# Moving the copy of one bank of finished accumulators from VectorE to ScalarE

## The chip, the cores and the metric

The kernel runs on one core of one Trainium2 chip. The metric is the device time of one execution in microseconds, shown as the median of several runs. Engines are named as in the profile: PE is TensorE's matmul stream and PEld its weight loads, DVE is VectorE, ACT is ScalarE, POOL is GpSimd, and SP issues DMAs.

## What is computed

The reference is a chunked linear recurrence (4 sequences, 8 heads, 768 positions, head width 32, state width 16), followed by a feed-forward block with the gate h * cos(h):

```python
# per chunk of positions, for each sequence and head
L = exp(cum[i] - cum[j]) * causal          # decays, cum = cumsum(log a)
y = ((C @ B.T) * L) @ x  +  (C @ state) * exp(cum)
state = exp(sum(la)) * state + sum_j B[j] x[j] * exp(cum[-1] - cum[j])

X = y.transpose(0, 2, 1, 3).reshape(3072, 256)
h = X @ w_in                                # 256 x 2048
out = (h * cos(h)) @ w_out                  # 2048 x 256
```

All inputs and outputs are float32.

## The kernel before

The 768 positions are cut into 6 chunks of 128. A chunk holds 4 x 128 = 512 tokens. The feed-forward block of a chunk takes 16 steps, numbered n = 16c + f through the whole kernel. A written-out loop over n sets the order of the instructions on every engine; there is no scheduler that would move them. From the second chunk on, the tokens of a chunk are handled in two turns of 8 steps, u = 0 and u = 1, each with half of the tokens and all of the 2048 inner columns.

Step n runs these parts, in this order:

- `first(n)`: 8 matmuls on TensorE form hp (L519), 128 x 512 in one PSUM bank; two banks are used in turn, so hp of step n+2 reuses the bank of step n. ScalarE computes k, the rounded number of turns (L523), and VectorE w = hp/(2 pi) - k (L525).
- `gate(n)`: ScalarE's sine (L530).
- `gated(n)`: VectorE's product gT = hp * cos (L535), which frees hp's bank. GpSimd then forms differences gd of it (`differ`, L560 to L563). Between gate and gated, and behind gated, VectorE has work for the scan of the next chunk: decays (L345) and masks (L436).
- the sums of a finished turn, if the step before ended one (`unsummed`, L633).
- `second(n - 2)`: from chunk 1 on this is `seven`: the product with w_out by seven half-size products in place of eight (L616). It is queued on TensorE behind hp of step n.

The seven products of a turn accumulate over 8 steps in two PSUM banks named o, called lo and hi. Products 1, 2 and 6 go to lo, products 7, 5, 4 and 3 to hi; a step issues them in the order 1, 2, 6, 7, 5, 4, 3. There are two buffers under the name o in all, so the next turn writes the same two banks, and its first step may write each only when it has been copied out. After the last step of a turn, lo is copied to the SBUF tile ps by ScalarE (L625) and hi by VectorE (L626). On ScalarE the next instruction is k of the next step; on VectorE it is w of the next step. The sums over ps (L633) and two output DMAs (L636) follow one step later, behind gated of that step.

There are 9 such ends of a turn: at steps 25, 33, 41 and so on up to 89 of the loop. The first chunk and the last turn of the last chunk finish in another way (L584; L648 and L661) and copy nothing with L625 or L626.

Of the kernel before, what the change touches and what calls it, by code (L numbers as in the profile page):

```python
# [25 lines left out]
def kernel(  # L26
# [30 lines left out]
    V, ACT, G, PE = nc.vector, nc.scalar, nc.gpsimd, nc.tensor  # L57
# [28 lines left out]
    def bank(shape, name, tag):  # L86
        return psum.tile(shape, FP32, tag=tag, bufs=2, name=name)

    def pair(name):

        return psum.tile([P, 2, 4 * P], FP32, tag="scan", bufs=2, name=name)
# [127 lines left out]
    for b in range(NB):  # L219
# [4 lines left out]
        out=a_in, in_=a.rearrange("(u b) h (c p) -> (b h c) u p", u=NU, p=P))  # L224
# [276 lines left out]
    hp, turns, gT, o = {}, {}, {}, {}  # L501
    NJ = NF // 2

    def turn_of(n):

        c, f = divmod(n, NF)
        return (f % 2, f // 2) if c == 0 else divmod(f, NJ)
# [59 lines left out]
    def second(n):  # L567
        c, f = divmod(n, NF)
        if c > 0:
            seven(n)  # L570
            return
        u, j = turn_of(n)
        if j == 0:
            o[c, u] = bank([P, 2, DM], "o", "o")
        g = gT.pop(n)
        for e in range(2):
            for t in range(2):
                PE.matmul(o[c, u][:, t], lhsT=g[:, 2 * e + t], rhs=w_out[:, 2 * j + e],  # L578
                          start=(j == e == t == 0), stop=(j == NJ - 1 and e == 1),
                          skip_group_check=True)  # L580
        if j < NJ - 1:
            return
        ob = conv.tile([P, 2, DM], FP32, tag="last", bufs=3, name="ob")
        (ACT.copy if u else V.tensor_copy)(out=ob, in_=o[c, u])  # L584
        for s in range(2):
            nc.sync.dma_start(out=to_rows[2 * u + s, c], in_=ob[s * W:(s + 1) * W])

    def seven(n):

        c = n // NF  # L590
        u, j = turn_of(n)
        final = n >= NC * NF - NJ
        if j == 0:


            if final:
                lo, hi = (pair("o")[:, 0].rearrange("p (q m) -> p q m", m=P) for _ in range(2))
                mid = bank([P, 4, P], "o", "o")
                o[c, u] = (mid, lo, hi, {1: mid[:, 0], 6: mid[:, 1], 7: mid[:, 2], 5: mid[:, 3],
                                         2: lo[:, 0], 3: lo[:, 1], 4: hi[:, 0]})  # L600
            else:
                lo, hi = (bank([P, 4, P], "o", "o") for _ in range(2))
                o[c, u] = (lo, hi, {1: lo[:, 0], 6: lo[:, 1], 2: lo[:, 2], 7: hi[:, 0],
                                    5: hi[:, 1], 4: hi[:, 2], 3: hi[:, 3]})
        at = o[c, u][-1]
        g = gT.pop(n)
        if n == NC * NF - 1:
            last_step(g, *o[c, u][1:3])
            return
        d = gd.pop(n)  # L610
        w = {1: w4[:, j, 0, 0], 2: w4[:, j, 1, 0], 3: w4[:, j, 1, 1], 4: wd[3][:, j],
             5: wd[0][:, j], 6: wd[2][:, j], 7: wd[1][:, j]}
        a_ = {1: g[:, 0], 2: g[:, 2], 3: d[:, 3], 4: g[:, 3], 5: d[:, 0], 6: d[:, 2], 7: d[:, 1]}
        starts = (1, 2, 4) if final else (1, 7)
        for q in (1, 2, 6, 7, 5, 4, 3):
            PE.matmul(at[q], lhsT=a_[q], rhs=w[q], start=(j == 0 and q in starts),  # L616
                      stop=(j == NJ - 1), skip_group_check=True)
        if final and j == NJ - 2:
            shared(o[c, u][0])
        if j < NJ - 1:  # L620
            return

        sum_ = two.tile([P, 7, P], FP32, tag="sum", bufs=1, name="sum")
        ps = two.tile([P, 7, P], FP32, tag="ps", bufs=1, name="ps")
        ACT.copy(out=ps[:, 0:3], in_=o[c, u][0][:, 0:3])  # L625
        V.tensor_copy(out=ps[:, 3:7], in_=o[c, u][1])  # L626

        def rest():
            for dst, a_, b_ in ((sum_[:, 0:2], ps[:, 1:3], ps[:, 0:1]),
                                (sum_[:, 5:7], ps[:, 3:5], sum_[:, 0:1]),  # L630
                                (sum_[:, 3:5], ps[:, 5:3:-1], sum_[:, 5:6]),
                                (sum_[:, 2:3], ps[:, 6:7], sum_[:, 6:7])):
                V.tensor_tensor(out=dst, in0=a_, in1=b_.to_broadcast([P, dst.shape[1], P]),  # L633
                                op=ALU.add)
            for s in range(2):
                nc.sync.dma_start(out=to_rows[2 * u + s, c],  # L636
                                  in_=sum_[s * W:(s + 1) * W, 1:5].rearrange(
                                      "p (t h) m -> p t (h m)", t=2))

        unsummed.append(rest)  # L640
# [4 lines left out]
    def shared(mid):  # L645

        ps = two.tile([P, 7, P], FP32, tag="ps", bufs=1, name="ps")
        ACT.copy(out=ps[:, 0:4], in_=mid)  # L648
        add = dict(op=ALU.add)
        V.tensor_tensor(out=ps[:, 1], in0=ps[:, 1], in1=ps[:, 0], **add)  # L650
        V.tensor_tensor(out=ps[:, 4:6], in0=ps[:, 2:4],
                        in1=ps[:, 1:2].to_broadcast([P, 2, P]), **add)
        V.tensor_tensor(out=ps[:, 6], in0=ps[:, 4], in1=ps[:, 3], **add)

        shares_.update({0: ps[:, 0:6:5], 1: ps[:, 4:7:2]})

    def last_step(g, lo, hi):

        for t, acc in enumerate((lo, hi)):
            for e in range(2):  # L660
                PE.matmul(acc[:, 0:2], lhsT=g[:, 2 * e + t], rhs=w_out[:, NF - 2 + e],  # L661
                          start=False, stop=(e == 1), skip_group_check=True)
            ob = conv.tile([P, 2, P], FP32, tag="last", bufs=3, name="ob")
            V.tensor_tensor(out=ob, in0=acc[:, 0:2], in1=shares_[t], op=ALU.add)
            for s, eng in enumerate((nc.sync, nc.scalar)):
                eng.dma_start(out=to_rows[NB - 2 + s, NC - 1, :, t],
                              in_=ob[s * W:(s + 1) * W].rearrange("p h m -> p (h m)"))
# [28 lines left out]
    for dst, src in ((a_cut, cut), (a_all, la)):  # L696
        nc.sync.dma_start(
            out=dst.rearrange("(u b) h (c p) -> (b h c) u p", u=NU, p=P), in_=src)
# [63 lines left out]
    for n in range(NC * NF + LAG):  # L762
        c, f = divmod(n, NF)
# [75 lines left out]
```

## Time and profile before

| | |
|---|---|
| median of 4 runs | 380.81 us (380.80 to 381.57) |
| the profiled execution | 380.8 us, span 379.0 us, clock granted to TensorE 1.0 |
| TensorE busy | 373.1 us (98%) |
| VectorE busy | 279.9 us (74%) |
| ScalarE busy | 173.4 us (46%) |
| GpSimd busy | 213.4 us (56%) |
| copy of lo (L625, ACT, 128x384) | 9 x 0.458 us |
| copy of hi (L626, DVE, 128x512) | 9 x 0.679 us |
| a step of L519 on TensorE | 1.73 us for 8 matmuls |
| a step of L616 on TensorE | 1.56 us for 7 products (14 records), in most steps |

The span is the time from the first to the last instruction that the profile shows; the execution's own time has 1.8 us around it. A busy share is an average over the whole span. Matmuls overlap, so that the sum of their single durations is more than the time that a step takes. Times in the timeline count from the start of the span.

### The profile page before, as it was taken

The numbers are of one execution on the slowest core, as the hardware profiler recorded it, in microseconds if no ns is written. First come the engines' busy times: TensorE is split into PE (matmuls) and PEld (weight loads), VectorE is DVE, ScalarE is ACT, GpSimd is POOL, SyncE is SP. The second block draws the span as 40 slices with busy tenths as digits, with TensorE's granted clock in tenths as the row PEclk, the third lists the DMA queues.
The fourth block names the chain that finished last, engine by engine and source line by source line (L and its number), as shares of the span: only waits on it lengthen the run. The fifth ranks groups of instructions, "written<-read, shape, count | busy, mean of one in ns | idle before, by whom it ended". The sixth has DMA issues, their size and how long they took to land.

```text
span 379.0 us, 7680 instructions
## 1 busy us (share of the span) xinstructions
PE 373.1 (98%) x2980; PEld 330.2 (87%) x2980; DVE 279.9 (74%) x431; ACT 173.4 (46%) x303; POOL 213.4 (56%) x330
## 2 busy tenths in 40 slices
PE   8999999999999999999999999999999999999996
PEld 2578888889989999998999998899998999999995
DVE  8879999899689748967748986756986862554643
ACT  4877756444344434443434453424444433433442
POOL 6767565579864437673444683443675343454551
PEclk9999999999999999999999999999999999999999
DMA  7999889979230961420781340100010000010011
GB/s 82 264 257 272 244 215 134 166 99 170 82 108 19 150 59 58 136 74 2 85 71 55 83 122 6 42 2 2 1 30 3 9 20 2 0 29 0 2 28 29
DMA packets 106371, 30.42 MB, mean 80 GB/s; under 512 B 75520, under 2 KB 102240, under 8 KB 106336
## 3 DMA queue, kind: packets, MB, share of 16 engines
q1 hardware_dynamic: 106176, 29.81, 39.8%
q8 instruction: 23, 0.38, 0.5%
q10 hardware_dynamic: 160, 0.13, 0.1%
q14 instruction: 12, 0.10, 0.1%
HBM read 26.59 MB, written 3.34 MB: 79 GB/s over the span
## 4 chain that ended last, share of the span: by engine, by line
PE 96%; DVE 2%; POOL 1%; issue 0%; POOLq 0%
PE hp L519 43%; PE o L616 33%; PE o L578 7%; PE g L423 3%; PE y L457 3%; PE y L450 1%; PE tp L406 1%; PE a_ps L299 1%; PE warm L101 1%; PE g L374 1%; DVE mag L209 1%; POOL w_in L217 1%; PE o L661 1%; DVE mag L207 0%; PE s_ps L478 0%; PE l_ps L318 0%
## 5 line engine op out<-in xcount | busy, mean ns | idle before, releaser
L519 PE MATMUL hp<-yT,w_in 128*128 128x256 f32 x768 | 183.8, 382 | 0.6 <-POOL w_in L217 0.3
L519 PEld LDWEIGHTS hp<-yT,w_in 128*128 128x128 f32 x768 | 139.5, 190 | 21.5 <-issue 3.2
L560 POOL TENSOR_TENSOR gd<-gT 128x256 f32<-128x256 f32 x79 | 59.9, 758 | 104.9 <-DVE gT L535 79.5
L530 ACT ACTIVATE w<-w,quarter 128x512 f32<-128x512 f32 x96 | 69.3, 722 | 77.7 <-DVE w L525 77.5
L523 ACT ACTIVATE k<-hp 128x512 int32<-128x512 f32 x96 | 57.2, 596 | 103.7 <-PE hp L519 103.1
L525 DVE SCALAR_TENSOR_TENSOR w<-hp,k 128x512 f32<-128x512 f32 x96 | 65.7, 684 | 50.3 <-ACT k L523 50.1
L535 DVE TENSOR_TENSOR gT<-hp,w 128x512 f32<-128x512 f32 x96 | 65.2, 679 | 32.4 <-ACT w L530 27.2
L616 PE MATMUL o<-words,gd 128*128 128x128 f32 x474 | 66.9, 277 | 0.0
L616 PEld LDWEIGHTS o<-words,gd 128*128 128x128 f32 x474 | 59.8, 192 | 0.5
L345 DVE TENSOR_TENSOR_SCAN lam<-arow,unit 128x512 f32<-128x512 f32 x40 | 55.7, 1393 | 0.0
L563 POOL TENSOR_TENSOR gd<-gT,gd 128x128 f32<-128x128 f32 x79 | 48.1, 608 | 6.2
L616 PEld LDWEIGHTS o<-w_out,gT 128*128 128x128 f32 x316 | 46.9, 191 | 3.5
L616 PE MATMUL o<-w_out,gT 128*128 128x128 f32 x316 | 48.0, 274 | 0.0
L562 POOL TENSOR_TENSOR gd<-gT,gd 128x128 f32<-128x128 f32 x79 | 41.4, 524 | 6.2
L578 PE MATMUL o<-w_out,gT 128*128 128x256 f32 x128 | 30.3, 380 | 0.4 <-POOL w_out L217 0.4
L616 PE MATMUL o<-w_out,gd 128*128 128x128 f32 x158 | 30.6, 275 | 0.0
L616 PE MATMUL o<-words,gT 128*128 128x128 f32 x158 | 30.5, 275 | 0.0
L578 PEld LDWEIGHTS o<-w_out,gT 128*128 128x128 f32 x128 | 24.2, 190 | 4.0 <-POOL w_out L217 0.8
L436 DVE TENSOR_TENSOR m<-g,lam 128x512 f32<-128x512 f32 x40 | 25.6, 680 | 0.0
L616 PEld LDWEIGHTS o<-w_out,gd 128*128 128x128 f32 x158 | 24.0, 192 | 0.0
L616 PEld LDWEIGHTS o<-words,gT 128*128 128x128 f32 x158 | 24.0, 192 | 0.0
L633 DVE TENSOR_TENSOR sum<-ps,sum 128x256 f32<-128x256 f32 (+1 forms) x27 | 16.7, 645 | 0.6
(91 smaller groups left out, 281.3 us busy)
## 6 DMA issues: line engine op xcount, KB each, us to landing
arow<-a_cut SPq DMA_DIRECT2D x20, 512.0 KB, 4.0
words<-in_moe_w_in_dram SPq DMA_DIRECT2D x8, 512.0 KB, 5.6
words<-in_moe_w_out_dram SPq DMA_DIRECT2D x8, 512.0 KB, 8.8
out_dram<-sum SPq DMA_DIRECT2D x18, 128.0 KB, 2.5
xr<-in_x_dram SPq DMA_DIRECT2D x4, 512.0 KB
along<-a_all SPq DMA_DIRECT2D x20, 64.0 KB
xr<-in_x_dram SPq DMA_DIRECT2D x8, 128.0 KB
bc<-in_B_dram SPq DMA_DIRECT2D x4, 256.0 KB, 5.1
```

Of the source, the lines that this page charges most:

```text
L345: V.tensor_tensor_scan(out=lam[c, b][:, hs].rearrange("p h i -> p (h i)"), data0=rows_.rearrange("p h i -> p (h i)"), data1=unit.rearrange ...
L436: V.tensor_tensor(out=of[0], in0=g[q][:, :, s * 2 * P:(s + 1) * 2 * P], in1=of[1], op=ALU.mult)
L519: PE.matmul(to_[:, e], lhsT=w_in[:, k, fs], rhs=y[:, k, u], start=(k == 0), stop=(k == KT - 1), skip_group_check=True)
L523: ACT.activation(k, hp[n], AF.Copy, bias=0.25, scale=INV_2PI)
L525: V.scalar_tensor_tensor(out=w, in0=hp[n], scalar=INV_2PI, in1=k, op0=ALU.mult, op1=ALU.subtract)
L530: ACT.activation(cos, cos, AF.Sin, bias=quarter, scale=TWO_PI)
L535: V.tensor_tensor(out=gT[n], in0=hp.pop(n), in1=cos, op=ALU.mult)
L560: G.tensor_tensor(out=d[:, 0:2], in0=g[:, 1:2].to_broadcast([P, 2, P]), in1=g[:, 3::-3], op=ALU.subtract)
L562: G.tensor_tensor(out=d[:, 2], in0=g[:, 0], in1=d[:, 0], op=ALU.subtract)
L563: G.tensor_tensor(out=d[:, 3], in0=g[:, 2], in1=d[:, 2], op=ALU.subtract)
L578: PE.matmul(o[c, u][:, t], lhsT=g[:, 2 * e + t], rhs=w_out[:, 2 * j + e], start=(j == e == t == 0), stop=(j == NJ - 1 and e == 1), skip_gr ...
L616: PE.matmul(at[q], lhsT=a_[q], rhs=w[q], start=(j == 0 and q in starts), stop=(j == NJ - 1), skip_group_check=True)
```

## The change

The copy of hi is issued on ScalarE's queue right behind the copy of lo, and no longer on VectorE's queue. Shapes, tiles and the order of everything else stay. On TensorE, the product that first writes hi in the next turn (product 7) waits for ScalarE where it waited for VectorE; the order of instructions on TensorE, GpSimd and the DMA queue is unchanged. ScalarE has 9 instructions more, VectorE 9 fewer.

```diff
         sum_ = two.tile([P, 7, P], FP32, tag="sum", bufs=1, name="sum")
         ps = two.tile([P, 7, P], FP32, tag="ps", bufs=1, name="ps")
         ACT.copy(out=ps[:, 0:3], in_=o[c, u][0][:, 0:3])
-        V.tensor_copy(out=ps[:, 3:7], in_=o[c, u][1])
+        ACT.copy(out=ps[:, 3:7], in_=o[c, u][1])
 
         def rest():
```

## The prediction

> **What bounds the kernel now.** I read the page's busy shares and its chain by engine first, then the chain in order of time, then the timelines of single engines at the turn boundaries. The page says:
>
> ```profile
> PE 373.1 (98%) x2980; PEld 330.2 (87%) x2980; DVE 279.9 (74%) x431; ACT 173.4 (46%) x303; POOL 213.4 (56%) x330
> PE 96%; DVE 2%; POOL 1%; issue 0%; POOLq 0%
> ```
>
> TensorE is busy for 98% of the span and carries 96% of the chain, so the other engines matter only where they make TensorE wait. The nine copies that the change moves take 6.1 us of VectorE; taking them away is worth nothing by itself. The question is what TensorE loses to them. The chain in order of time (start, length, what) shows it:
>
> ```profile
> 113.23 1.56 PE o L616 x14
> 114.79 1.73 PE hp L519 x8
> 116.52 1.73 PE o L616 x14
> ...
> 148.28 1.71 PE o L616 x14
> ...
> 208.22 1.67 PE o L616 x14
> ...
> 327.57 1.56 PE o L616 x14
> ```
>
> One step of the second product (L616, 7 products recorded as 14 matmuls) takes 1.56 us. The first step after a finished turn takes more: 1.73 at 116.52, 176.46, 236.35 and 296.25, 1.71 at 148.28, 1.67 at 208.22 and 268.12. At 327.57 and 353.89, the last two of the nine boundaries, it takes 1.56. Where inside the step the time goes, TensorE's weight loads show, an ordinary step first and the step after the first boundary second:
>
> ```profile
> 113.40 0.75 PEld L616 LDWEIGHTS o<-words,gd 128*128 128x128 f32 x6
> ...
> 116.69 0.92 PEld L616 LDWEIGHTS o<-words,gd 128*128 128x128 f32 x6
> ```
>
> The six loads are two each for products 6, 7 and 5. Product 7 is the first to write the second bank, which the copy of L626 must have emptied. VectorE and ScalarE at that boundary:
>
> ```profile
> 115.76 0.68 DVE L535 TENSOR_TENSOR gT<-hp,w 128x512 f32<-128x512 f32 x1
> 116.36 0.68 DVE L626 COPY ps<-o 128x512 f32<-128x512 f32 x1
> 117.24 0.69 DVE L525 SCALAR_TENSOR_TENSOR w<-hp,k 128x512 f32<-128x512 f32 x1 [0.20 <-ACT k L523]
> ```
> ```profile
> 114.68 0.72 ACT L530 ACTIVATE w<-w,quarter 128x512 f32<-128x512 f32 x1 [0.76 <-DVE w L525]
> 115.31 0.46 ACT L625 COPY ps<-o 128x384 f32<-128x384 f32 x1
> 116.61 0.60 ACT L523 ACTIVATE k<-hp 128x512 int32<-128x512 f32 x1 [0.84 <-PE hp L519]
> ```
>
> The turn's last matmul ends at 114.79. ScalarE empties its bank by 115.77. VectorE is still busy with masks and the product gT, begins its copy only at 116.36 and ends at 117.04. The load of product 7 starts at 117.09, 0.05 later; by the spacing of the loads (0.11) it would have started at 116.91. At all seven long boundaries that load starts about 0.05 behind the end of L626. At 327.57 the copy ends at 327.84, 0.12 ahead of the load, and nothing is lost.
>
> **The change part by part.**
>
> *Removed from VectorE:* 9 copies of 0.68 us. VectorE's next instruction, w (L525), starts at 117.24, 0.03 after ScalarE's k ended (116.61 + 0.60), and so at each boundary: it waits for k, not for VectorE. Nothing on that chain comes earlier: 0. The sum below takes no gain from VectorE's free time.
>
> *Added to ScalarE:* 9 copies of 128x512 from a bank of accumulators. The nearest row is ScalarE's own copy of the same kind in the last turn (L648), 0.587 us; the other 128x512 ScalarE copies are 0.565 (L584) and 0.588 (L465), and the longest 128x512 instruction on ScalarE is the sine, 0.722. I take 0.587, the same tiles and shape, with 0.565 and 0.722 as ends. L625 starts 0.09 before the sine ahead of it ends (114.68 + 0.72 against 115.31), so the new copy starts at 115.31 + 0.46 - 0.09 = 115.68 and ends at 116.27 (116.24 to 116.40). Its bank was complete at 114.79, so it does not wait.
>
> *What is queued behind it:* k of the next step (L523), which now has 0.84 us of idle time before it, waiting for hp. The new copy takes 0.587 - 0.09 = 0.50 of that (0.47 to 0.63). k still waits for hp, with 0.34 us over (0.21 at the upper end). The idle time is 0.84 or 0.85 at all nine boundaries. Cost 0. Were that cover gone, k, w, the sine and gT would each be late by the excess.
>
> *The wait that moves:* product 7 now waits for ScalarE's second copy instead of VectorE's. It needs the release at 116.91 - 0.05 = 116.86; it comes at 116.27, 0.59 ahead (0.46 at the upper end). The seven waits go: 4 x 0.17 + 0.15 + 2 x 0.11 = **1.05 us** of TensorE's time, all on the chain. The last two boundaries gain nothing.
>
> *The readers of the copies* (the sums of L633) run one step later, from 119.56: 3 us of cover. The single buffer ps was last read by sums some eight steps (over 20 us) earlier. GpSimd's and the DMA queue's instructions keep their order; the output DMAs follow the sums, which follow gT of the step after the boundary, as before.
>
> *What is late next.* TensorE comes 0.11 to 0.17 us earlier against a VectorE that behind each boundary is set by work fed from before the wait (k of the next step comes from an hp finished before product 7). So I looked for the tightest hand-over to TensorE in the steps behind a boundary. In the step after next, gT (L535) ends at 155.98 and the load of the hp that reuses its bank starts at 156.29: 0.31, and 0.28 at the two like places later. GpSimd's difference (L562) ends at 158.18, and its reader's load starts at 158.47: 0.29 (0.25 later). These lie behind the second, fourth and sixth boundaries, where TensorE gains 0.15, 0.11 and 0.11. After taking that off and 0.05 for the hand-over, 0.09 to 0.12 us are left. Behind the other boundaries with a gain the margins are over 1 us. So nothing is given back, but there it is close.
>
> VectorE's copy starts 1.05 us after ScalarE's (116.36 against 115.31), since it stands behind other work. Against the change speaks the Trainium skill's page "TensorEngine Tiling (Array Packing)", section PSUM Bottleneck: it advises emptying PSUM with both ScalarE and VectorE. By that rule both copies would begin together at 115.31, the second bank would be free at 115.99, and two ScalarE copies in a row would free it 0.28 us later; both ends lie before 116.86, so that the time would stay at 380.8. The row shows that they do not begin together, and I go by the row.
>
> *Sum.* The profiled execution took 380.8 us, its span 379.0 and 1.8 around it; the median of the four runs is 380.81, so the two agree. 380.80 - 1.05 = **379.75 us**, 0.28% less. Faster or slower is told from no change at 0.2%, or 0.76 us, about what a measurement of this kernel can tell.
>
> **The rivals.**
>
> *Part of it is given back.* The margins of 0.09 to 0.12 us behind the second, fourth and sixth boundaries rest partly on GpSimd's ends, which are rough. If they are gone, TensorE waits there instead and 0.15 + 0.11 + 0.11 = 0.37 us return: 380.80 - 0.68 = 380.12, within 0.2%. For it: these are the smallest margins of the steady part. Against it: no wait of TensorE there is in the trace, and 0.05 is what a hand-over took.
>
> *The wait has another cause.* If the load of product 7 is held by something that ends with L626 by chance, the time stays: 380.8. Against it: behind waits of three sizes, all seven ends of L626 lie about 0.05 ahead of the load, and where L626 is early there is no wait.
>
> *Slower: the second copy is long.* ScalarE's copy would have to take over 116.86 - 115.68 = 1.18 us for the wait to return. It then returns at all nine boundaries, 9 x (D - 1.18); at D = 1.30 all of the 1.05 is lost, and at D = 1.38 the kernel is at 380.80 - 1.05 + 1.80 = 381.55, slower by 0.2%. For it: two engines would read accumulators at once (gT reads hp at 115.76). Against it: that holds for L625 too, which takes 0.458 beside a VectorE mask from the accumulators and the same where VectorE reads none for half of it, and 1.38 is 2.3 times the row.
>
> **How the numbers follow.** Forecast 0.77, partly given back 0.10, no effect 0.06, long copy 0.07. That makes faster 0.77, same 0.16, slower 0.07. The forecast's own spread is small: runs of one kernel repeat to 0.02 us but for one that was 0.8 above, the 1.05 is a sum of rows rounded to 0.01, and the ends of the copy's duration change nothing. Below, 379.5 allows 0.25 us for waits I did not count; above, the range takes in the case given back, with the same allowance: 379.5 to 380.4.
>
> **What would show it.** In the changed profile, L616 steps at all nine boundaries take 1.56 us in the chain; the load groups of products 6, 7 and 5 take 0.75; ScalarE has 9 copies of about 0.59 on L626, right behind L625, and about 0.34 us of idle time ahead of the next k; VectorE's busy time falls by 6.1 us and its idle time grows as much; TensorE's busy time and the span fall by about 1 us. The prediction is wrong if L626 on ScalarE ends after the load of product 7 could go, if k's idle time is gone, or if TensorE gets waits for gT or gd (L535, L562) two steps behind a boundary.

## The result and the profile after

The changed kernel takes 380.45 us (median of 32 runs, 379.71 to 381.43), the kernel before 381.57 us (median of 53 runs, 380.67 to 382.22). The ratio is 0.9972, with a 95% interval of 0.9966 to 0.9978: faster by 0.28%, or 1.07 us. The difference is the one that was forecast (1.05 us, 0.28%); the time is not: 379.75 was forecast with a range to 380.4, and the measured median lies 0.05 us above that range. The four runs of before that the forecast started from, at 380.80 to 381.57 with three of them at 380.8, were near the fast end of what this kernel does.

The page of the changed kernel, with the span and the busy shares:

```profile
span 379.3 us, 7680 instructions
PE 373.3 (98%) x2980; PEld 329.8 (87%) x2980; DVE 274.7 (72%) x422; ACT 177.0 (47%) x312; POOL 213.6 (56%) x330
```

The profiled execution took 381.2 us with a span of 379.3, which is longer than the 379.0 of before. The span alone hides the gain, so I cut it at the first hp matmul (L519). It starts at 17.49 us in the profile of before and at 18.79 in that of after; from there to the end it is 361.53 us before and 360.47 after, 1.06 less. The first hp, before and after:

```profile
17.49 2.29 PE L519 MATMUL hp<-yT,w_in 128*128 128x256 f32 x8 [0.32 <-POOL w_in L217]
```
```profile
18.79 2.29 PE L519 MATMUL hp<-yT,w_in 128*128 128x256 f32 x8 [0.31 <-POOL w_in L217]
```

This stretch is the measure used below. The later start is not the change's doing (see the repeated runs).

The chain of work in order of time, after, at the first, second, fourth and eighth boundary (start, length, what):

```profile
117.81 1.56 PE o L616 x14
...
149.40 1.56 PE o L616 x14
...
209.01 1.56 PE o L616 x14
...
327.80 1.56 PE o L616 x14
```

Every boundary step now takes 1.56 us. The weight loads of products 6, 7 and 5 at the first boundary, and ScalarE there:

```profile
117.98 0.75 PEld L616 LDWEIGHTS o<-words,gd 128*128 128x128 f32 x6
```
```profile
115.97 0.72 ACT L530 ACTIVATE w<-w,quarter 128x512 f32<-128x512 f32 x1 [0.76 <-DVE w L525]
116.60 0.46 ACT L625 COPY ps<-o 128x384 f32<-128x384 f32 x1
116.96 0.59 ACT L626 COPY ps<-o 128x512 f32<-128x512 f32 x1
117.90 0.60 ACT L523 ACTIVATE k<-hp 128x512 int32<-128x512 f32 x1 [0.36 <-PE hp L519]
```

The group of loads takes 0.75 where it took 0.92. The copy of hi starts 0.36 us behind the start of L625, takes 0.59 and ends at 117.55, 0.65 ahead of the load that needs its bank (118.20). k still waits for hp, and 0.36 us of idle time are left ahead of it.

Step by step against the profile of before, with both set to zero at the first hp matmul, TensorE gains 0.174, 0.147, 0.172, 0.109, 0.173, 0.109 and 0.173 us at the first seven boundaries, together 1.057, and nothing anywhere else.

### The profile page after: what moved, and what is told of

Same layout as the page of the kernel before. It is cut to its first block, busy times and chain, and to the rows that moved or that the text cites. A ratio compares the mean times of both kernels' runs of the same rounds, so it can differ in the third digit from the quotient of the medians.

```text
span 379.3 us, 7680 instructions
## 1 busy us (share of the span) xinstructions
PE 373.3 (98%) x2980; PEld 329.8 (87%) x2980; DVE 274.7 (72%) x422; ACT 177.0 (47%) x312; POOL 213.6 (56%) x330
## 4 chain that ended last, share of the span: by engine, by line
PE 96%; POOL 1%; DVE 1%; ACT 1%; issue 0%; POOLq 0%
PE hp L519 43%; PE o L616 33%; PE o L578 7%; PE g L423 3%; PE y L457 3%; PE y L450 1%; PE a_ps L299 1%; PE tp L406 1%; PE warm L101 1%; PE g L374 1%; PE o L661 1%; PE s_ps L478 0%; PE l_ps L318 0%; PE tp L360 0%; PE y L391 0%; DVE mag L209 0%
## 5 line engine op out<-in xcount | busy, mean ns | idle before, releaser
L519 PE MATMUL hp<-yT,w_in 128*128 128x256 f32 x768 | 183.8, 382 | 0.6 <-POOL w_in L217 0.3
L519 PEld LDWEIGHTS hp<-yT,w_in 128*128 128x128 f32 x768 | 139.4, 190 | 21.5 <-issue 2.9
L616 PE MATMUL o<-words,gd 128*128 128x128 f32 x474 | 65.8, 275 | 0.0
L616 PEld LDWEIGHTS o<-words,gd 128*128 128x128 f32 x474 | 59.3, 192 | 0.0
L345 DVE TENSOR_TENSOR_SCAN lam<-arow,unit 128x512 f32<-128x512 f32 x40 | 56.0, 1400 | 0.0
L563 POOL TENSOR_TENSOR gd<-gT,gd 128x128 f32<-128x128 f32 x79 | 47.3, 599 | 6.2
L616 PEld LDWEIGHTS o<-w_out,gT 128*128 128x128 f32 x316 | 46.9, 191 | 3.6
L616 PE MATMUL o<-w_out,gT 128*128 128x128 f32 x316 | 48.0, 274 | 0.0
L616 PE MATMUL o<-words,gT 128*128 128x128 f32 x158 | 30.6, 275 | 0.0
L616 PE MATMUL o<-w_out,gd 128*128 128x128 f32 x158 | 30.6, 275 | 0.0
L616 PEld LDWEIGHTS o<-words,gT 128*128 128x128 f32 x158 | 24.0, 192 | 0.0
L616 PEld LDWEIGHTS o<-w_out,gd 128*128 128x128 f32 x158 | 24.0, 192 | 0.0
```

Source lines behind the costliest of these rows:

```text
L345: V.tensor_tensor_scan(out=lam[c, b][:, hs].rearrange("p h i -> p (h i)"), data0=rows_.rearrange("p h i -> p (h i)"), data1=unit.rearrange ...
L519: PE.matmul(to_[:, e], lhsT=w_in[:, k, fs], rhs=y[:, k, u], start=(k == 0), stop=(k == KT - 1), skip_group_check=True)
L563: G.tensor_tensor(out=d[:, 3], in0=g[:, 2], in1=d[:, 2], op=ALU.subtract)
```

## The experiments

Theory 1 is the prediction's: only the time at which hi is released counts, and TensorE's 1.05 us of waits is all there is. The rivals: VectorE's free time brings the gain; ScalarE's time costs something; the changed kernel starts later. The edits are against the kernel before (e2, e3, e4, e7) or the changed kernel (the rest).

Each ratio is to runs of the kernel before that were taken beside it, so the level of before differs a little from row to row (medians 381.14 to 381.69 in the experiments).

| run | ratio to before (95%) | first hp at, us | stretch from there, us |
|---|---|---|---|
| before | | 17.49 | 361.53 |
| after | 0.9972 (0.9966 to 0.9978) | 18.79 | 360.47 |
| e7_before, repeated | 1.0007 (0.9997 to 1.0016) | 17.75 | 361.44 |
| e8_after, repeated | 0.9978 (0.9969 to 0.9987) | 17.98 | 360.48 |
| e1_refill | 0.9979 (0.9968 to 0.9990) | 17.74 | 360.37 |
| e2_early | 0.9983 (0.9974 to 0.9993) | 18.87 | 360.69 |
| e3_both_dve | 1.0118 (1.0098 to 1.0138) | 17.45 | 366.06 |
| e4_split | 0.9963 (0.9950 to 0.9976) | 17.87 | 360.37 |
| e5_twice | 0.9995 (0.9984 to 1.0006) | 17.50 | 361.32 |
| e6_three | 1.0118 (1.0093 to 1.0143) | 17.70 | 365.89 |
| e9_no_fill | 1.0014 (1.0001 to 1.0026) | 18.93 | 360.46 |

In e1, e4 and e7 the stretch is 0.1 us shorter than in other profiles with the same boundaries; e3 has 0.17 and e6 0.25 of the same kind. It arises at one place, the hp of step 2 at about 23 us, long before the first boundary, and is left out of the readings below.

### Both kernels repeated

No edit.

> The kernel before, unchanged, once more. Measure: the stretch from the first hp matmul (L519) to the end of the span, 361.53 us in the profile of before and 360.47 in that of after, and the start of that first matmul, 17.49 and 18.79. Theory 1 (the change takes 1.05 us of waits out of the steady part; the start varies from run to run whatever the kernel): the stretch is 361.53 within 0.05, the first hp starts anywhere between about 17.4 and 19, and the ratio to the kernel before is 1.000. Theory 2 (the later start belongs to the changed kernel): the first hp starts at 17.5 again.

> The changed kernel, once more. Theory 1: the stretch from the first hp matmul to the end is 360.47 within 0.05; the first hp starts anywhere between about 17.4 and 19; ratio to before about 0.997. Theory 2 (the later start belongs to the changed kernel): the first hp starts at 18.8 again.

The stretch repeats: 361.44 and 360.48, the first 0.04 outside the 0.05 that had been allowed (the 0.1 us at step 2, above). In this pair, whose starts lie closer together, the span falls from 379.2 to 378.5 us and TensorE's busy time from 373.4 to 372.5, the fall of about 1 us that the first two profiles hide. The first hp came at 17.75 and 17.98, so the late start of the profile of after was that execution's, not the kernel's. Theory 2 of these two runs is out.

### VectorE kept as busy as before

```diff
         ACT.copy(out=ps[:, 3:7], in_=o[c, u][1])
+        spare = conv.tile([P, TB], FP32, tag="last", bufs=3, name="spare")
+        V.tensor_copy(out=spare, in_=done[n + LAG])   # done[n]: hp of step n
```

> The changed kernel, and VectorE makes a copy of 128x512 that nobody reads, from the bank of hp into a spare tile, in the place where its copy of hi was: VectorE is as busy as before. Theory 1 (only the time at which hi is released counts): the stretch from the first hp matmul to the end stays at 360.5, VectorE's busy time goes back up by 6.1 us, all nine boundary steps of L616 at 1.56. Rival (the gain comes from VectorE's free time): the stretch goes back to about 361.5.

VectorE's timeline at the first boundary has the useless copy where the copy of hi had been, of the same length:

```profile
115.89 0.68 DVE L536 TENSOR_TENSOR gT<-hp,w 128x512 f32<-128x512 f32 x1
116.49 0.68 DVE L629 COPY spare<-hp 128x512 f32<-128x512 f32 x1
117.38 0.69 DVE L525 SCALAR_TENSOR_TENSOR w<-hp,k 128x512 f32<-128x512 f32 x1 [0.21 <-ACT k L523]
```

w still waits for k behind it. VectorE is busy for 280.1 us, as before (279.9), and the stretch is 360.37, or 360.47 without the 0.1 at step 2: the whole gain is there. VectorE's time was worth nothing.

### The split kept, VectorE's copy ahead of gT

```diff
+            if ends_turn(n):          # n = 25, 33, ..., 89
+                second(n - LAG)
             gated(n)
...
-        if n >= LAG:
+        if n >= LAG and not ends_turn(n):
             second(n - LAG)
```

The sums of the turn are still held back for one step.

> The kernel before with its split between ScalarE and VectorE, but VectorE's copy of hi is issued ahead of the product gT (L535) of the same step and not behind it. Theory 1: the copy starts at about 115.76 in place of 116.36 and ends 0.4 us before product 7 needs the bank; the waits go, the stretch from the first hp matmul to the end is 360.5, as in the changed kernel, though ScalarE does nothing more and VectorE nothing less. Rival (moving work to ScalarE is what helps): 361.5. gT is 0.6 us later at nine steps; its readers have over 2 us there, so nothing is lost by that.

```profile
117.14 0.68 DVE L626 COPY ps<-o 128x512 f32<-128x512 f32 x1
117.74 0.68 DVE L535 TENSOR_TENSOR gT<-hp,w 128x512 f32<-128x512 f32 x1
```

The two instructions have changed places, all nine boundary steps of L616 take 1.56 us, and the stretch is 360.69. So the engine that copies does not matter for this wait; the place in its queue does. The expected 360.5 was missed by 0.2: TensorE loses 0.06, 0.05 and 0.10 us at the hp of steps 37, 53 and 69, the tight hand-overs that the prediction had named. At the first of these places GpSimd, now later, runs beside the sums, whose first takes 0.57 instead of 0.41, and gT of step 35 is 0.11 late behind them, with 0.05 of room (see e5 below). That nothing would be lost by the later gT was wrong.

### Both copies on VectorE

```diff
-        ACT.copy(out=ps[:, 0:3], in_=o[c, u][0][:, 0:3])
+        V.tensor_copy(out=ps[:, 0:3], in_=o[c, u][0][:, 0:3])
```

> The kernel before, and VectorE copies lo too, ahead of hi. Theory 1: lo is released about 0.55 us after VectorE gets to it (116.36 at the first boundary), while product 1 wants it at 116.14; wait 0.76 to 0.82 at seven boundaries and about 0.57 at the last two, 6.7 us in place of 1.05; the stretch from the first hp matmul to the end is 361.5 + 5.65 = 367.2. If the wait for hi were all that counts, and lo had slack, it would be the 0.46 us by which hi is later at nine boundaries: about 365.

TensorE's loads at the first boundary:

```profile
116.77 0.52 PEld L616 LDWEIGHTS o<-w_out,gT 128*128 128x128 f32 x4 [0.84 <-DVE ps L625]
117.21 0.75 PEld L616 LDWEIGHTS o<-words,gd 128*128 128x128 f32 x6
```

The wait is for lo now, and it stands at all nine boundaries. Against the changed kernel TensorE loses 0.71 us at four of them, 0.65 at three and 0.46 at the last two, 5.7 together, not the 6.7 expected. The load did come 0.82 us late, as said (at 116.77; e3 runs 0.19 ahead, so that the 116.14 stands for 115.95). But the first load of a step usually stands 0.22 us ahead of the second, where the later ones follow at 0.11; here the second follows it at 0.11, so that this much of its wait costs nothing. The other figure, 365, came from a copy of hi that is late by 0.46 with lo unharmed; the loads say that lo is what waits.

### hi shared

```diff
-        V.tensor_copy(out=ps[:, 3:7], in_=o[c, u][1])
+        ACT.copy(out=ps[:, 3:5], in_=o[c, u][1][:, 0:2])
+        V.tensor_copy(out=ps[:, 5:7], in_=o[c, u][1][:, 2:4])
```

> The kernel before, and hi is shared: ScalarE copies its first half behind lo, VectorE the second half where it copied all of hi. Theory 1: VectorE's half takes 0.42 us and ends at 116.78 at the first boundary, 0.08 before product 7 needs the release at 116.86; no wait, the stretch from the first hp matmul to the end is 360.5. Rival (the gain goes with the VectorE time that is taken away, of which this is 0.26 of 0.68 us): about 361.1.

```profile
116.63 0.42 DVE L627 COPY ps<-o 128x256 f32<-128x256 f32 x1
```
```profile
116.96 0.75 PEld L616 LDWEIGHTS o<-words,gd 128*128 128x128 f32 x6
```

The half ends at 117.05, 0.13 before the load of product 7 (116.96 + 2 x 0.11 = 117.18), and nothing waits. The stretch is 360.37 (360.47 without the 0.1 at step 2), the whole gain with 0.26 of the 0.68 us removed. It is not told apart from the changed kernel.

### ScalarE's copy made twice and three times

```diff
         ACT.copy(out=ps[:, 3:7], in_=o[c, u][1])
+        ACT.copy(out=ps[:, 3:7], in_=o[c, u][1])     # e6: two such lines
```

> The changed kernel with ScalarE's copy of hi made twice. Theory 1 (a release is needed at 116.86 at the first boundary, k has 0.84 us of cover): the second copy ends at 116.77, so no wait for hi; k (L523) is 0.07 us late at the nine boundaries, within the 0.09 to 0.12 us left behind the tightest three: the stretch from the first hp matmul to the end stays at 360.5, at most 360.7. Rival (ScalarE's time is on the path): 9 x 0.50 = 4.5 us more, 365.

> The changed kernel with ScalarE's copy of hi made three times. Theory 1: the third copy ends at 117.27 at the first boundary, so product 7 waits 0.41 us at all nine boundaries, 3.7 us; k is 0.57 late, TensorE itself 0.41; the stretch from the first hp matmul to the end is 364.2. Rival (ScalarE's time is on the path): 9 x 1.0 = 9 us more, 369.5.

Twice: the load of product 7 comes only 0.01 us late, 0.05 behind the end of the second copy, and TensorE loses nothing there; and yet 0.85 us are lost, most of the gain. TensorE loses 0.28, 0.27 and 0.28 us at the hp of steps 37, 53 and 69 and nowhere else. Its load there, in e5:

```profile
156.27 1.38 PEld L519 LDWEIGHTS hp<-yT,w_in 128*128 128x128 f32 x7 [0.20 <-PE o L616]
```

The wait is put down to TensorE there, but what the load needs is gT of step 35, two steps back on the same bank. VectorE's timeline of e5, from w of step 34 on:

```profile
149.00 0.69 DVE L525 SCALAR_TENSOR_TENSOR w<-hp,k 128x512 f32<-128x512 f32 x1 [1.02 <-ACT k L523]
149.60 1.40 DVE L345 TENSOR_TENSOR_SCAN lam<-arow,unit 128x512 f32<-128x512 f32 x1
150.92 0.66 DVE L535 TENSOR_TENSOR gT<-hp,w 128x512 f32<-128x512 f32 x1
...
155.49 0.66 DVE L535 TENSOR_TENSOR gT<-hp,w 128x512 f32<-128x512 f32 x1
```

and of the changed kernel:

```profile
150.12 0.69 DVE L525 SCALAR_TENSOR_TENSOR w<-hp,k 128x512 f32<-128x512 f32 x1 [0.87 <-ACT k L523]
150.73 1.22 DVE L345 TENSOR_TENSOR_SCAN lam<-arow,unit 128x512 f32<-128x512 f32 x1
151.86 0.67 DVE L535 TENSOR_TENSOR gT<-hp,w 128x512 f32<-128x512 f32 x1
...
156.44 0.66 DVE L535 TENSOR_TENSOR gT<-hp,w 128x512 f32<-128x512 f32 x1
```

e5 runs 1.28 us ahead here. With that put right, w is 0.16 us late, the scan adds 0.18, and gT of step 35 is 0.33 late. In the changed kernel gT ends at 157.10 and the load is at 157.26, 0.16 later; but a hand-over takes 0.12 of that, for wherever TensorE waits for gT at these steps, in e2, e5 and e6, the load starts 0.12 behind its end (here 156.15 and 156.27). So the room was 0.05, and the other 0.28 is what TensorE loses. The expectation was wrong in three ways: a second ScalarE copy to the same tile begins 0.62 us behind the first, not 0.50, so k is 0.15 late and not 0.07; the scan is stretched; and the room is 0.05, not 0.09 to 0.12.

Three times: product 7 waits at eight boundaries, 0.62 us each (0.41 had been expected; the two repeats are 0.12 later each). The load of product 7 in e6, and the chain that leads to it:

```profile
117.52 0.52 PEld L616 LDWEIGHTS o<-words,gd 128*128 128x128 f32 x4 [0.54 <-ACT ps L628]
```
```profile
115.38 0.37 ACT ps L625
115.75 0.49 ACT ps L626
116.24 0.02 issue
116.26 0.59 ACT ps L627
116.86 0.02 issue
116.88 0.59 ACT ps L628
117.47 0.04 issue
117.52 1.16 PE o L616 x8
```

The load starts 0.05 us behind the end of the last copy. At the ninth boundary there is no wait for hi: the turn behind it is the last one, whose products 1, 6, 7 and 5 go to the bank that lo had, and the others to further banks; its load of product 7 starts 0.58 us before the last copy of hi ends. The hp of step 93 then loses 0.39, where 0.49 us lie between gT and the load in the changed kernel. Of the 5.67 us lost behind step 2 against the changed kernel, 4.95 are the eight waits, and the rest is about 0.1 at each of the hp of steps 37, 53 and 69; 9.0, the price if ScalarE's time were on the path, is not reached.

### No idle matmuls at the start

```diff
     warm = bank([P, 4, P], "warm", "o")
-    fill(warm, 2)
```

> The changed kernel without the two idle matmuls that open TensorE's work (from 1.06 us of the span on); TensorE's first work then comes at about 4.5. In the ten profiles so far TensorE's clock reaches its full rate between 3.97 and 7.20 us of the span, 2.9 to 6.1 after TensorE's first work, and the first hp starts between 17.45 and 18.87, about 0.45 us later for each us by which the clock is late. Theory 1 (this ramp is what makes the runs differ by up to 1.5 us): the clock is full at 7.4 to 10.7 us, the first hp starts at 18.9 to 20.5, and the stretch from there to the end stays at 360.5; the median rises by 1 to 2 us against the changed kernel. Rival (the start varies with the loads): the first hp starts at 17.4 to 18.9 as before.

The four scan matmuls that open the work proper (a_ps, L299), in before, after and e9, one fence each:

```profile
4.52 1.08 PE L299 MATMUL a_ps<-a0s,those 128*64 128x512 f32 x4
```
```profile
4.77 1.97 PE L299 MATMUL a_ps<-a0s,those 128*64 128x512 f32 x4
```
```profile
4.49 1.97 PE L299 MATMUL a_ps<-a0s,those 128*64 128x512 f32 x4 [4.49 <-DVE fro L267]
```

The trace's first record of the granted clock, full rate, stands at 4.21 us in before, 7.03 in after and 7.69 in e9. The same matmuls take 0.59 to 0.64 us each behind that point and 1.06 to 1.11 ahead of it. Without the fill the clock is full at 7.69 and the first hp comes at 18.93, both as expected though near the early end; the stretch is 360.46. The rows also tell where the later start of after comes from: in the chain, TensorE's second pair of transposes (L360) stands at 8.69 us in before and at 9.99 in after, 1.30 later, and the first hp is 1.29 later: nothing is added in between. The median is 381.92 us, and the ratio to before 1.0014 against 0.9978 of the repeated changed kernel, 1.4 us more. The rival expected a start of 17.4 to 18.9, and 18.93 is only just above that; the clock's record and the median speak against it.

The Trainium skill's page "TensorE: Matmul & The Clock Gate", section Part 1 (the HAM clock gate), says that the clock rises after about 3.4 us of sustained work, in a window that runs freely, so that the cold phase differs from run to run. The rows agree as to the spread: in the ten profiles with the fill the clock is full 2.9 to 6.1 us after TensorE's first matmul. As to the length they agree only roughly: in three of these ten, and in e9 with 3.2 us, it took less than the page's 3.4.

## Why the prediction was right or wrong

- **The wait that moves: right.** Seven waits were to go, 4 x 0.17 + 0.15 + 2 x 0.11 = 1.05; measured 1.057, at those places. e1, e2 and e4 give the same with VectorE as busy as before, with the split kept, and with a shorter copy.
- **Added to ScalarE: right.** 0.59 us for the copy (0.587 taken), 0.36 us of idle time left ahead of k (0.34 said).
- **Removed from VectorE, worth 0: right**, shown by e1. Its busy time fell by 5.2 us, not 6.1: each copy overlapped the instruction ahead of it by 0.08, and the page counts such time once; the scans (L345) took 0.3 us more, 56.0 against 55.7.
- **What is late next: right that nothing is given back, but the margin was mis-sized.** 0.16 us were left between gT and the load at 157.26, as said (0.31 - 0.15). But the 0.05 taken off for the hand-over is what the load of product 7 needs behind a copy; behind gT it is 0.12 (e2, e5, e6), where the trace has an instruction that waits for VectorE just ahead of the load. So about 0.05 us was left at these three places, not 0.09 to 0.12, and e2 and e5 overran it.
- **The sum's level: wrong.** This is the step that failed: "the median of the four runs is 380.81, so the two agree", and with it "runs of one kernel repeat to 0.02 us but for one that was 0.8 above". Four runs were taken for the kernel's level, and the one that differed for the odd one out. The 53 runs have a median of 381.57 and a range of 1.55 us; only 6 of them took 380.82 or less, and three of these stood among the four, which was chance. With that median the same sum gives 381.57 - 1.05 = 380.52; measured 380.45. The profile of before was a fast start (first hp at 17.49; 17.45 to 18.87 in ten profiles), so its time was a low one to subtract from. The upper end of the range allowed 0.25 us on top of the case given back; the spread of the start alone is 1.4.
- **The rival of the long copy: it left out a path.** It set the loss at a copy of over 1.18 us, by the wait for hi alone, at nine boundaries. The turning point was right: the two copies of e5 take 1.20 together, and the load of product 7 is 0.01 late. But there are eight boundaries (e6), and at that point e5 has already lost 0.85 us through k, the scan and gT. By the prediction's own 0.84 us of cover, k is late from a copy of 0.84 + 0.09 = 0.93 us on; the rival did not count that. The two rivals are one: what is late on ScalarE comes out at the tight hand-over.
- **The rule of two engines** (the page "TensorEngine Tiling (Array Packing)", section PSUM Bottleneck), as the prediction worked it out, would have left the time as it was. Here two engines pay only where both reach their copy in time: e2 and e4 use both, the changed kernel one, and all three are free of the wait; the split in its old place was not.

## What to carry to other kernels

When TensorE is the bound, look for the step that is longer than its like, and ask which queue position releases what it waits for: moving a copy to where it starts sooner removes the wait, whichever engine makes it. Before subtracting from a level, see how far the runs of that kernel spread, and cut the trace at a point behind the part that varies; the stretch behind it repeated to 0.1 us where whole runs spread over 1.5.

## What the runs showed of the hardware

- **The start of the clock sets the spread.** In ten profiles the first hp starts at 17.45 us when the clock is full at 3.97, and at 18.87 when it is full at 7.20: 0.44 us for each us. That is about what matmuls at half rate lose: by the lengths above, a us ahead of that point does the work of 0.6 / 1.08 = 0.56 us. The other eight lie on that line within 0.09. In all eleven traces the full-rate record lasts a whole number of steps of 3.413 us (372.05, 375.47 or 378.88 us: 109, 110 or 111 steps). If full rate can begin anywhere within one such step, whole runs can differ by 0.44 x 3.41 = 1.5 us, an estimate from these rows; the 53 runs range over 1.55. The profile's clock column shows full rate ahead of the first record, so that the ramp is seen only in the matmuls' lengths.
- **VectorE's scan and GpSimd delay each other, and who is first decides.** In the changed kernel the scan (L345) starts at 150.73 and takes 1.22 while GpSimd's L563, begun at 150.74, takes 1.45. In e5 L563 starts first, at 149.46, and takes 0.46; the scan, from 149.60, takes 1.40. Whoever is first keeps its length: the next scan of the changed kernel, at 155.31 with GpSimd idle, takes 1.21. 0.15 us of lateness elsewhere turned the order round. The Trainium skill's page "SBUF — State Buffer", section Who interferes with whom, says that an instruction of VectorE with two SBUF inputs, as this scan is, contends with one of GpSimd that reads SBUF, and that the order of issue decides who blocks; the lengths agree with that.
- **A repeated ScalarE copy to the same part of a tile starts 0.62 us behind the start of the last one**, 0.03 after its end, where a copy to another part of the tile starts 0.10 before its forerunner ends (116.96 against 117.06). In the trace of e6 the repeated copy waits for a semaphore that ScalarE's own instructions raise, and the first copy of hi does not; so it is the program's order of the two writes that costs the overlap. A repeated copy to another tile was not tried.
